# Joining the weighings of four tiles, with buffers moved between the stages, in a top-k attention and channel-mix kernel on one Trainium2 core

## The chip, the cores and the metric

The kernel runs on one core of one Trainium2 chip. A core has five engines with a queue of instructions each: TensorE (PE, matrix products and transpositions; the loading of its stationary operand is shown apart as PEld), VectorE (DVE), ScalarE (ACT), GpSimd (POOL) and SyncE (SP, which here only issues DMAs). Each engine works through its own queue in order and waits on semaphores for the others. The metric is the device time of one launch in microseconds (us); lower is better. Times are medians of several runs; the profile is of one execution.

## The reference, cut to what matters

```python
B, H, S, D = 8, 8, 576, 64          # batches, heads, positions, width of a head
scores = (q @ k.T) / sqrt(D)        # 576 x 576 for each of 64 heads
kth    = the 32nd largest of each row
scores = where(scores >= kth, scores, -1e9)
attn   = exp(scores - max);  attn = attn / (sum(attn) + 1e-9)
x      = attn @ v                   # heads side by side: 8 x 576 x 512

x_prev = x, one position later, zero first
xk = mu_k * x + (1 - mu_k) * x_prev
xr = mu_r * x + (1 - mu_r) * x_prev
h  = relu(xk @ w_k) ** 2            # 512 -> 1024
r  = 1 / (1 + exp(-(xr @ w_r)))     # 512 -> 512
out = r * (h @ w_v)                 # 1024 -> 512
```

All arrays are float32. Every matrix product of the second half is made from three products of a high and a low part (`three`, lines 703 to 705).

## The kernel before, in words

**Tiles.** Two heads are worked on together. Their 1152 rows of scores are nine tiles of 128 rows: tiles 0 to 7 hold 128 rows each of one head (even tiles the first head, odd ones the second), tile 8 the last 64 rows of both. There are 8 batches x 4 pairs of heads x 9 = 288 tiles. A batch goes over its four pairs of heads twice: first tiles 0 to 3 of each pair, then tiles 4 to 8 (`HALVES`), so there are 64 visits. The turned keys `K` of a pair are held from the first visit to the second (`HOLD`, four buffers).

**A tile's way.** PE multiplies turned queries with `K` (`score`, L990, and `sliver`, L986, which is the product with the last 64 keys; tile 8 has `score8`, L977 and L978). ACT copies the scores out of PSUM (`keep`, L995). DVE looks for the 24 largest (`cand`, `best`, `drop`: L1000, L1002, L1005) and writes two bounds into `seen` (`under`, L1012). ACT compares the scores with the bound (`count`, L1020), POOL multiplies (`below`, L1022), DVE takes the next eight (`eighth`, L1023) and from them the 32nd score (`nine`, L1025, also into `seen`). ACT makes the exponentials (L1028), and DVE masks and sums them (L1031, into `E`). PE turns `E` (`turn`, four transpositions, L1036), ACT copies the result into `et` (L1038). For every two tiles the last columns are turned together (`turnl`, L1045) and copied into `el` (L1047).

**Weighing.** `weigh` (L1066, L1067) multiplies `et` and `el` of two tiles with the values: ten products on half of the array's columns each time, for a pair of tiles. It follows every second tile, and tile 8 by itself: 160 weighings. Where `PAIR` is true, the two weighings of a group of four tiles are made as one piece of work. After a group, `place` (L1101, L1103) scales the result with the turned inverse of the sums and writes it to `xT`.

**Last keys.** The last 64 keys and, on a second visit, the last 64 queries are loaded to `tl`, turned together (L948: one transposition on a first visit, two on a second) and copied to `kd` (L950), at every visit.

**Mix.** The 4608 rows of all batches are 18 chunks of 256. For each chunk and for both mixes (k first, then r) POOL subtracts and adds (`change` L1173, `add` L1183), ACT scales (`share` L1178) and rounds to the high parts `xh` (L1185), and POOL makes the low parts `xl` (L1187, two instructions, for half of the channels each). PE then makes, in this strict order, 96 products `hidden` (256 columns, read `xl` of mix k), 24 products `gate` (512 columns, read `xl` of mix r) and 48 products `value`. POOL also squares and splits the hidden rows (L1206, L1207).

**Order.** All instructions are put in order at build time by a planner: a list of work per engine, a table of offsets by name (`OFF`, with `HEAD` and `TAIL` for the first and last tiles), costs of changing between kinds of work on PE (`SWITCH`, `LEAVE`), and the buffers of each kind (`sizes`, `MORE`). On the chip only the order and the waits are left. `seen` has two buffers, one for each of two batches; `lowest` (L1110) reads a batch's `seen` at its end.

**Weights.** In the first tiles all weights are brought in and split into high and low parts (`weight`, L1273 and on), with 80 DVE instructions in all.

## Time and profile before

| | |
|---|---|
| median of 3 runs | 1239.97 us (1239.73 to 1240.59) |
| the profiled execution, its own time | 1239.58 us |
| its span in the profile | 1238.0 us |
| busy: PE, DVE, ACT, POOL | 1185.3, 1132.4, 1107.8, 980.6 us |

The span runs from the first to the last instruction of the program; the execution's own time also holds what lies around it, 1.6 us. A busy time is the sum of what an engine works on; ends of matrix products are modelled, so that PE's busy time overlaps its own next instruction, and what PE is worth in time is read from the starts of its instructions.

### The profile page before, as it was taken

How to read it: one execution, taken by the hardware profiler on the slowest of the kernel's cores; microseconds unless marked ns; L12 is line 12 of the kernel's file. 1: busy time of each engine (PE TensorE's matmuls, PEld its weight loads, DVE VectorE, ACT ScalarE, POOL GpSimd, SP SyncE). 2: the span in 40 equal slices, each digit the busy share in tenths (PEclk: the TensorE clock that was granted, in tenths of full speed). 3: DMA queues.
4: the chain of work that ended last, by engine and by line, in shares of the span. 5: the costliest groups of instructions: out<-in, count | busy, mean ns of one | idle time of the engine just before them, and what ended most of it. 6: DMA issues, size and time to landing. Idle time of an engine off the chain costs nothing.

```text
span 1238.0 us, 29646 instructions
## 1 busy us (share of the span) xinstructions
PE 1185.3 (96%) x9069; PEld 913.8 (74%) x9069; DVE 1132.4 (91%) x6217; ACT 1107.8 (89%) x2428; POOL 980.6 (79%) x872
## 2 busy tenths in 40 slices
PE   5876999999999999999999999999999999999997
PEld 3434777878777776778787877787878787878786
DVE  5999999999999999999999999999989998999711
ACT  6897899999999999999999999999999999999752
POOL 2568995887778877888789787979697969788895
PEclk8997799999999999999999999999999999999999
DMA  7233112111221122111121112111211121101000
GB/s 189 93 95 97 35 35 66 41 36 42 57 54 31 45 50 57 36 39 45 50 56 38 35 49 58 42 43 34 59 47 45 27 59 40 50 26 32 20 27 20
DMA packets 125512, 61.80 MB, mean 50 GB/s; under 512 B 101792, under 2 KB 118176, under 8 KB 125344
## 3 DMA queue, kind: packets, MB, share of 16 engines
q1 hardware_dynamic: 124656, 59.42, 17.8%
q8 instruction: 74, 1.21, 0.4%
q14 instruction: 94, 0.77, 0.2%
q10 hardware_dynamic: 688, 0.39, 0.1%
HBM read 50.34 MB, written 9.44 MB: 48 GB/s over the span
## 4 chain that ended last, share of the span: by engine, by line
PE 79%; DVE 9%; ACT 6%; issue 1%; POOL 0%; DMA 0%; SPq 0%; DVEq 0%; ACTq 0%
PE rot L703 13%; PE rot L705 12%; PE rot L704 12%; PE ps L1066 10%; PE rot L1036 9%; PE ps L990 9%; PE ps L986 2%; PE ps L1067 2%; PE ps L977 2%; PE rot L934 2%; DVE cand L1000 2%; DVE E L1031 2%; PE rot L1088 1%; ACT sc L995 1%; PE ps L1045 1%; ACT se L1028 1%
## 5 line engine op out<-in xcount | busy, mean ns | idle before, releaser
L1022 POOL TENSOR_TENSOR sg<-sc,sg 128x576 f32<-128x576 f32 x288 | 409.2, 1423 | 165.6 <-ACT sg L1020 161.9
L1000 DVE MAX8 cand<-sc 128x8 f32<-128x82 f32 (+1 forms) x2016 | 390.5, 231 | 10.6 <-ACT sc L995 9.9
L1020 ACT ACTIVATE sg<-sc,seen 128x576 f32<-128x576 f32 x288 | 225.9, 784 | 8.6 <-DVE seen L1012 7.2
L1031 DVE SCALAR_TENSOR_TENSOR E<-sc,seen,se 128x576 f32<-128x576 f32 x288 | 231.0, 802 | 0.5 <-DVE nine L1025 0.2
L1028 ACT ACTIVATE se<-sc,seen 128x576 f32<-128x576 f32 x288 | 217.6, 756 | 8.4 <-DVE E L1031 5.8
L1023 DVE MAX8 top<-sg 128x8 f32<-128x576 f32 x288 | 215.7, 749 | 9.7 <-POOL sg L1022 9.2
L995 ACT ACTIVATE sc<-ps 128x576 f32<-128x576 f32 x288 | 185.4, 653 | 27.8 <-DVE E L1031 11.4
L1036 PE MATMUL rot<-ident,E 128*128 128x128 f32 x1152 | 180.7, 280 | 12.7 <-DVE E L1031 5.1
L1038 ACT ACTIVATE et<-rot 128x512 f32<-128x512 f32 x288 | 173.9, 604 | 9.7 <-PE rot L1036 8.6
L1002 DVE MAX8 top<-cand 128x8 f32<-128x56 f32 x864 | 179.7, 208 | 2.1
L1036 PEld LDWEIGHTS rot<-ident,E 128*128 128x128 f32 x1152 | 133.4, 143 | 62.6 <-DVE E L1031 7.1
L703 PE MATMUL rot<-xh,wk 128*128 128x256 f32 x576 | 172.5, 299 | 0.4 <-ACT kd L950 0.4
L1066 PEld LDWEIGHTS ps<-et,v 128*64 128x64 f32 x2560 | 128.7, 138 | 54.5 <-ACT el L1047 17.9
L1066 PE MATMUL ps<-et,v 128*64 128x128 f32 (+1 forms) x2560 | 164.4, 271 | 3.0 <-ACT el L1047 2.7
L705 PE MATMUL rot<-xh,wk 128*128 128x256 f32 x576 | 162.4, 282 | 0.0
L704 PE MATMUL rot<-xl,wk 128*128 128x256 f32 x576 | 162.1, 281 | 0.0
L990 PE MATMUL ps<-K,qs 64*128 64x512 f32 x512 | 149.7, 662 | 0.7 <-ACT sc L995 0.6
L703 PE MATMUL rot<-wv,hh 128*128 128x512 f32 x288 | 123.3, 428 | 0.0
L1005 DVE MATCH_REPLACE8 cand<-top,cand 128x56 f32<-128x56 f32 x576 | 115.9, 201 | 0.0
L705 PE MATMUL rot<-wv,hl 128*128 128x512 f32 x288 | 113.7, 395 | 0.0
L704 PE MATMUL rot<-wv,hh 128*128 128x512 f32 x288 | 113.6, 394 | 0.0
L703 PEld LDWEIGHTS rot<-xh,wk 128*128 128x128 f32 x576 | 109.7, 190 | 5.0 <-issue 2.4
(115 smaller groups left out, 2723.0 us busy)
## 6 DMA issues: line engine op xcount, KB each, us to landing
v<-in_v SPq DMA_DIRECT2D x64, 256.0 KB, 2.8
out<-eb SPq DMA_DIRECT2D x35, 256.0 KB, 2.0
kn<-in_k SPq DMA_DIRECT2D x64, 128.0 KB, 2.8
qn<-in_q SPq DMA_DIRECT2D x126, 64.0 KB, 2.1
stage<-in_moe_w_k SPq DMA_DIRECT2D x8, 512.0 KB, 6.2
xT<-in_moe_w_v SPq DMA_DIRECT2D x8, 512.0 KB, 3.6
tl<-in_k SPq DMA_DIRECT2D x128, 16.0 KB, 2.0
vr_in<-in_v SPq DMA_DIRECT2D x128, 16.0 KB, 2.5
```

The costliest lines, as they stand in the source:

```text
L703: return [nc.tensor.matmul(ps, lhsT=sh, rhs=mh, start=first, stop=False), nc.tensor.matmul(ps, lhsT=sh, rhs=ml, start=False, stop=False), ...
L704: nc.tensor.matmul(ps, lhsT=sh, rhs=ml, start=False, stop=False),
L705: nc.tensor.matmul(ps, lhsT=sl, rhs=mh, start=False, stop=last)]
L990: return [nc.tensor.matmul(ps[h].t, lhsT=qs.t[w, c * 128:(c + 1) * 128], rhs=P.K.t[w], start=True, stop=True) for h, w in enumerate(ws)]
L1000: lambda T=T, c=c: nc.vector.max(T.cand.t[:, 8 * c:8 * c + 8], T.sc.t[:, CUTS[c]:CUTS[c + 1]]), reads=[T.sc], writes=[(T.cand, c)])
L1020: lambda T=T, sn=sn: nc.scalar.activation(T.side.t, T.sc.t, AF.Sign, bias=sn(T, 1), scale=-BELOW, accum_out=T.top.t[:, TOPK:TOPK + 1]),
L1022: plan.op(POOL, "below", n, 1375, 1430, lambda T=T: nc.gpsimd.tensor_mul(T.side.t, T.sc.t, T.side.t), reads=[T.sc], writes=[T.side])
L1023: plan.op(DVE, "eighth", n, 660, 754, lambda T=T: nc.vector.max(T.top.t[:, 24:32], T.side.t), reads=[T.side], writes=[(T.top, 3)])
L1028: plan.op(ACT, "exps", n, 667, 754, lambda T=T, pe=pe, sn=sn: nc.scalar.activation(pe.t, T.sc.t, AF.Exp, bias=sn(T, 0), scale=SCALE), read ...
L1031: lambda T=T, U=U, pe=pe, sn=sn: nc.vector.scalar_tensor_tensor(T.e(), T.sc.t, sn(T, 2), pe.t, op0=OP.is_ge, op1=OP.mult, accum_out=U.rs.t ...
L1036: return [nc.tensor.transpose(pt.t[:, c * 128:(c + 1) * 128], E.t[:, o + c * 128:o + (c + 1) * 128], ident) for c in range(NKC)]
L1066: return [*[nc.tensor.matmul(pa[hs[j]], lhsT=vs[j][:, c, :], rhs=ms[c][j], start=(c == 0), stop=False) for c in range(NKC) for j in range(2)],
```

## The change

1. `PAIR` is true: both weighings of a group of four tiles are one piece of work, so 96 pieces in place of 160, of the same 1600 products.
2. `MORE`: `et` has five buffers in place of three, `el` three in place of two; `xl` one in place of two, `seen` one in place of two. 
3. The last 64 keys are turned once, on a pair's first visit, and held in 128 more columns of `K`; `kd` is one buffer for the last queries alone. A second visit turns and copies the queries only, and no keys are loaded on it.
4. The tables of the planner are other numbers throughout (`OFF`, `HEAD`, `TAIL`, `BONUS`, `NEAR` and others).
5. The branch for `n < WCL`, which is never taken as `WCL` is 0, is written in another way, and the constant `floor` for it is gone, one memory set on POOL.

```diff
-OFF = dict(kt=-21.382, kq=-14.248, rest=-18.039, v=-7.011, v8=8.546, tk=-6.103, ck=5.233, tq=-5.229, cq=-6.609, tr=-1.299, cr=-10.196, zero=24.959,
+OFF = dict(kt=-30.36, kq=-8.949, rest=-15.609, v=-10.829, v8=2.951, tk=-6.086, ck=4.079, tq=-5.255, cq=-6.6, tr=-1.056, cr=-7.948, zero=32.08,
...
-PAIR = False
+PAIR = True
...
-FULL = "sc", "K", "kd", "et", "el", "sg", "qs", "xm", "r", "eb", "lb", "ri"
-MORE = dict(xh=2, xl=2, et=3, top=3, el=2, qn=2, K=1 + HOLD)
+FULL = "sc", "kd", "et", "el", "sg", "qs", "xm", "r", "eb", "lb", "ri"
+MORE = {'xh': 2, 'xl': 1, 'et': 5, 'top': 3, 'el': 3, 'qn': 2, 'K': 4, 'seen': 1}
...
-            P.tl, P.kd, P.K = buf("tl"), buf("kd"), held.pop((b, hp), None)
+            P.K = held.pop((b, hp), None)
             fresh = P.K is None
+            lasts = [(k, 0)] * fresh + [(q, 128)] * full
+            P.tl, P.kd = buf("tl") if lasts else None, buf("kd") if full else None
...
-            pt, m = buf("rot"), 1 + full
-
-            def turn_t(P=P, pt=pt, m=m):
-                return [nc.tensor.transpose(pt.t[:, i * 128:(i + 1) * 128], P.tl.t[:, i * 128:(i + 1) * 128], ident) for i in range(m)]
...
+            for x, o in lasts:
+                pt, dst, last = buf("rot"), P.kd if o else P.K, "r" if o else "w"
...
-        sizes = dict(kn=(1, [128, NKC, 2, D]), qn=(1, [128, 2, 2, D]), tl=(1, [128, 256]), v=(1, [128, 2, NKC, D]), K=(2, [128, MAIN]), kd=(2, [128, 256]),
+        sizes = dict(kn=(1, [128, NKC, 2, D]), qn=(1, [128, 2, 2, D]), tl=(1, [128, 256]), v=(1, [128, 2, NKC, D]), K=(2, [128, MAIN + 128]), kd=(1, [128, 128]),
```

The tables move instructions on every engine; three places show how. In the changed kernel's rows the line numbers are one higher from `attend` on (L1067 and L1068 are the weighing, L1188 is `xl`, L1013 is `under`, L1024 is `eighth`).

PE, in the middle of the program, before: each weighing (eight products on two `et`, two on `el`) stands by itself between transpositions, scores and products of the mix.

```order
L1036 MATMUL rot2_155<-ident_59,E0_116 128x128 x4
L1066 MATMUL ps_151<-et1_123,v0_92 64x128
L1066 MATMUL ps_151<-et2_124,v0_92 64x128
...
L1067 MATMUL ps_151<-el1_126,vr_in_75 64x128 x2
L948 MATMUL rot1_154<-ident_59,tl0_91 128x128 x2
L703 MATMUL rot2_155<-wr0_70,xh1_133 128x512
...
L986 MATMUL ps_151<-kd0_97,qs0_99 128x2x64
L1045 MATMUL ps_151<-ident_59,E0_116 128x128
L990 MATMUL ps_151<-K0_93,qs0_99 128x512 x2
L1066 MATMUL ps_151<-et0_122,v0_92 64x128
L1066 MATMUL ps_151<-et1_123,v0_92 64x128
```

PE, the same part of the program, now:

```order
L705 MATMUL rot1_153<-wr0_70,xl0_135 128x512
L1067 MATMUL ps_150<-et2_122,v0_92 64x128
L1067 MATMUL ps_150<-et3_123,v0_92 64x128
...
L1068 MATMUL ps_150<-el0_125,vr_in_75 64x128 x2
L1067 MATMUL ps_150<-et4_124,v0_92 64x128
L1067 MATMUL ps_150<-et0_120,v0_92 64x128
...
L1068 MATMUL ps_150<-el1_126,vr_in_75 64x128 x2
L703 MATMUL rot1_153<-wr0_70,xh1_134 128x512
```

The second weighing of a group has moved up to the first one's end, and one change of work into a weighing and one out of it are gone.

POOL, in the last but one chunk, where `hidden` (96 products) and `gate` follow each other on PE with nothing between, before: `xl0` belongs to mix k, `xl1` to mix r, and `r` and `hl` are the hidden rows' squares and low parts.

```order
L1187 TENSOR_TENSOR xl0_134<-xm1_131,xh0_132 128x512
L1187 TENSOR_TENSOR xl1_135<-xm0_130,xh1_133 128x512
L1183 TENSOR_TENSOR xm1_131<-xm1_131,xT1_145 128x512
L1173 TENSOR_TENSOR xd00_128<-xT1_145 128x512
L1187 TENSOR_TENSOR xl1_135<-xm1_131,xh1_133 128x512
L1183 TENSOR_TENSOR xm0_130<-xm0_130,xT1_145 128x512
L1206 TENSOR_TENSOR r0_136<-r0_136 128x512
```

POOL, the same chunk, now:

```order
L1207 TENSOR_TENSOR r0_136<-r0_136 128x512
L1208 TENSOR_TENSOR hl_1325<-r0_136,hh_1287 128x512
L1207 TENSOR_TENSOR r1_137<-r1_137 128x512
L1188 TENSOR_TENSOR xl0_135<-xm0_131,xh1_134 128x512
L1188 TENSOR_TENSOR xl0_135<-xm1_132,xh1_134 128x512
L1208 TENSOR_TENSOR hl_1325<-r1_137,hh_1287 128x512
```

Both low parts of mix r stood ahead of the first hidden rows, and now stand behind the squares of the third of four, in the buffer that `hidden` reads to its end.

DVE, at the end of the fifth batch (`lowest` is the instruction that writes `least`), before: bounds of the next batch (into `seen1`) and its first `nine` and mask stand ahead of `lowest`.

```order
L1012 TENSOR_TENSOR seen1_115<-top1_108,se_152 128x2
L1000 MAX cand0_105<-sc2_103 128x8 x4
L1025 SCALAR_TENSOR_TENSOR nine0_112,seen1_115<-se_152,top0_107 128x9
L1002 MAX top2_109<-cand0_105 128x8
L1031 SCALAR_TENSOR_TENSOR E0_116,rs0_118<-sc0_101,seen1_115,se_152 128x576
...
L1012 TENSOR_TENSOR seen1_115<-top2_109,se_152 128x2
L1000 MAX cand1_106<-sc3_104 128x8 x4
L1110 TENSOR_REDUCE least_73<-seen0_114 128x1
L1002 MAX top0_107<-cand1_106 128x8
L1023 MAX top1_108<-sg1_111 128x8
```

DVE, the end of the fifth batch, now:

```order
L1003 MAX top2_108<-cand0_104 128x8
L1001 MAX cand1_105<-sc3_103 128x8 x2
L1111 TENSOR_REDUCE least_73<-seen0_113 128x1
L1013 TENSOR_TENSOR seen0_113<-top0_106,se_151 128x2
L1013 TENSOR_TENSOR seen0_113<-top1_107,se_151 128x2
L1013 TENSOR_TENSOR seen0_113<-top2_108,se_151 128x2
L1102 TENSOR_TENSOR xT0_144<-ps_150,ri0_128 128x256
L1024 MAX top0_106<-sg0_109 128x8
L1026 SCALAR_TENSOR_TENSOR nine0_111,seen0_113<-se_151,top0_106 128x9
```

The bounds of three tiles of the next batch have moved behind `lowest`, and the first `eighth` follows them with one `place` between.

## Rows read from the trace of the kernel before

**Rows 1.** The page of the profile: busy time of each engine (share of the span, instructions), and the span in 40 slices of 31 us, busy tenths of PE and DVE and the granted TensorE clock in tenths of full speed.

```profile
PE 1185.3 (96%) x9069; PEld 913.8 (74%) x9069; DVE 1132.4 (91%) x6217; ACT 1107.8 (89%) x2428; POOL 980.6 (79%) x872
...
PE   5876999999999999999999999999999999999997
...
DVE  5999999999999999999999999999989998999711
...
PEclk8997799999999999999999999999999999999999
```

**Rows 2.** Busy time by stretch: the first 36 tiles, then 18 tiles at a time (cut at every 18th mask on DVE). Columns: the stretch, its length, busy us (instructions) of PE, PEld, DVE, ACT and POOL, the granted clock, the DMA share and GB/s.

```profile
0.00:197.70 197.70, 157.39 (x968) 102.66 (x968) 182.64 (x888) 165.50 (x348) 134.32 (x124) 0.89 0.32 89
197.70:265.50 67.80, 66.54 (x522) 51.37 (x521) 66.32 (x375) 64.39 (x143) 54.86 (x49) 1.00 0.19 49
265.50:333.80 68.30, 67.37 (x561) 52.34 (x559) 67.73 (x395) 65.36 (x149) 55.23 (x51) 1.00 0.16 40
333.80:399.70 65.90, 65.46 (x515) 50.42 (x515) 64.81 (x372) 62.62 (x140) 53.76 (x47) 1.00 0.18 46
399.70:472.50 72.80, 72.30 (x596) 55.65 (x595) 70.82 (x401) 66.99 (x152) 58.20 (x56) 1.00 0.18 48
472.50:537.50 65.00, 63.80 (x490) 49.19 (x490) 63.65 (x367) 61.82 (x138) 52.02 (x45) 1.00 0.17 43
537.50:607.60 70.10, 69.74 (x575) 55.00 (x575) 69.39 (x401) 67.34 (x151) 57.19 (x54) 1.00 0.17 45
607.60:675.90 68.30, 68.02 (x530) 52.45 (x528) 67.15 (x379) 66.94 (x150) 59.13 (x50) 1.00 0.19 49
675.90:743.80 67.90, 67.25 (x546) 53.12 (x542) 66.16 (x379) 65.31 (x145) 56.70 (x51) 1.00 0.16 43
743.80:815.40 71.60, 71.39 (x576) 55.98 (x576) 68.94 (x381) 67.40 (x150) 58.78 (x54) 1.00 0.20 51
815.40:885.90 70.50, 70.30 (x578) 55.77 (x573) 68.31 (x392) 64.55 (x143) 53.49 (x49) 1.00 0.16 43
885.90:957.10 71.20, 71.20 (x567) 56.91 (x566) 67.80 (x378) 66.66 (x148) 60.24 (x53) 1.00 0.19 48
957.10:1027.10 70.00, 70.00 (x573) 55.90 (x571) 68.50 (x394) 66.60 (x151) 57.38 (x53) 1.00 0.16 40
1027.10:1102.10 75.00, 75.00 (x577) 59.06 (x576) 68.58 (x383) 68.85 (x151) 61.88 (x53) 1.00 0.15 41
1102.10:1166.90 64.80, 64.80 (x531) 51.90 (x531) 60.84 (x331) 59.14 (x131) 55.02 (x51) 1.00 0.09 26
```

**Rows 3.** The timeline of PE around one weighing and around transpositions, from answers of narrow windows (so that rows of the same products begin at several places): start, us until the last of them ends, the products, and how many rows. A product of two half-columns is two rows. The first row is four transpositions with others ahead of them, the next two rows are transpositions that follow each other; then comes a weighing with what stands ahead of it and behind it, and the copy on ACT that waits for its end.

```profile
601.40 0.60 PE L1036 MATMUL rot<-ident,E 128*128 128x128 f32 x4
...
608.45 0.27 PE L948 MATMUL rot<-ident,tl 128*128 128x128 f32 x1
608.56 0.38 PE L934 MATMUL rot<-ident,qn 128*128 128x128 f32 x2
...
605.20 0.27 PE L1045 MATMUL ps<-ident,E 128*128 128x128 f32 x1
605.40 1.09 PE L1066 MATMUL ps<-et,v 128*64 128x128 f32 x16
606.21 0.28 PE L1066 MATMUL ps<-et,v 128*64 128x128 f32 x2
606.43 0.28 PE L1067 MATMUL ps<-el,vr_in 128*64 128x128 f32 x2
606.64 0.65 PE L1036 MATMUL rot<-ident,E 128*128 128x128 f32 x4
606.76 0.28 ACT L1047 ACTIVATE el<-ps 128x128 f32<-128x128 f32 x1 [0.31 <-PE ps L1067]
```

**Rows 4.** Groups of instructions by line: count | busy us, mean ns of one | idle time of the engine just before them, and what ended most of it.

```profile
L948 PE MATMUL rot<-ident,tl 128*128 128x128 f32 x96 | 23.0, 294 | 0.8 <-ACT et L1038 0.6
...
L950 ACT ACTIVATE kd<-rot 128x256 f32<-128x256 f32 x32 | 12.4, 388 | 0.9 <-PE rot L948 0.6
L950 ACT ACTIVATE kd<-rot 128x128 f32<-128x128 f32 x32 | 8.9, 279 | 2.1 <-PE rot L948 1.9
...
L1066 PE MATMUL ps<-et,v 128*64 128x128 f32 (+1 forms) x2560 | 164.4, 271 | 3.0 <-ACT el L1047 2.7 <-DMA v<-in_v 0.2
L1101 DVE TENSOR_TENSOR xT<-ps,ri 128x256 f32<-128x256 f32 x64 | 26.6, 416 | 3.2 <-PE ps L1067 0.9 <-POOL xm L1183 0.8 <-PE ps L1045 0.6
L1020 ACT ACTIVATE sg<-sc,seen 128x576 f32<-128x576 f32 x288 | 225.9, 784 | 8.6 <-DVE seen L1012 7.2 <-DVE top L1023 0.7
L1022 POOL TENSOR_TENSOR sg<-sc,sg 128x576 f32<-128x576 f32 x288 | 409.2, 1423 | 165.6 <-ACT sg L1020 161.9 <-DVE rs L1078 1.2
L1187 POOL TENSOR_TENSOR xl<-xm,xh 128x512 fp32r<-128x512 f32 x72 | 92.4, 1288 | 9.2 <-ACT xh L1185 8.7
```

**Rows 5.** The timeline of PE where `hidden` ends and `gate` begins, in the last but one chunk.

```profile
1186.35 0.28 PE L705 MATMUL rot<-xh,wk 128*128 128x256 f32 x1
1186.46 0.40 PE L703 MATMUL rot<-wr,xh 128*128 128x512 f32 x1
1186.70 0.40 PE L704 MATMUL rot<-wr,xh 128*128 128x512 f32 x1
1186.93 0.40 PE L705 MATMUL rot<-wr,xl 128*128 128x512 f32 x1
```

More of the change, by code (lines that the diff above doesn't have):

```diff
@@ L46 @@
-CANDS, BESTS = 0.045, -0.62
-LAG, STEP, WAT, WSTEP, GATE, VALUE, PACE = 10.811, 15.812, 0.678, 0.755, 7.749, 14.045, -2.0
+OFF = dict(kt=-30.36, kq=-8.949, rest=-15.609, v=-10.829, v8=2.951, tk=-6.086, ck=4.079, tq=-5.255, cq=-6.6, tr=-1.056, cr=-7.948, zero=32.08,
+           score=-0.239, score8=-20.241, keep=-1.227, cand=5.068, best=-4.94, drop=-38.448, under=-2.732, nb=8.16, count=2.281, below=1.036,
+           eighth=6.204, nine=7.952, exps=2.736, mask=1.619, turn=3.274, et=4.281, turnl=3.599, el=4.345, weigh=1.315, inv=-0.179, inv2=-2.049,
+           turni=-0.717, ri=1.545, place=-0.114, lowest=16.268, ranks=15.011, mu=-9.72, nmu=11.088, changek=11.181, sharek=-4.663, addk=-17.151,
+           xhk=-0.124, xlk=-36.256, changer=-14.501, sharer=13.216, addr=3.351, xhr=6.025, xlr=-10.909, hidden=2.112, relu=-16.109, sq=3.703,
+           r2=7.857, hl=-4.972, gate=2.109, gexp=3.719, ga=14.142, ln=-0.365, inv1=3.697, newton=-7.448, value=0.016, scaled=-11.324, gated=-14.688,
+           store=6.787, w=19.186, wabs=-0.791, wclamp=0.38, wshift=-12.234, wsign=-0.223, wexp=-0.608, wfine=1.734, whi=4.534, wmul=13.044,
+           wsub=-11.3, wlo=2.053, spread=3.6, sliver=-2.225, low=1.195, lowt=-15.053, lowr=-7.264, lowc=-4.621, wcp=4.081, tw=-1.316, cw=-5.326)
@@ L78 @@
 WINDOW, PHASE, WARM, COLD = 3413.0, 2079.0, 0.87, 0.58
-NEAR = dict(PE=182, ACT=165, DVE=28, POOL=271, SP=294)
+NEAR = dict(PE=179, ACT=165, DVE=70, POOL=255, SP=502)
 LAST, JOINT, PEAT = "last", True, 112
-LWAT, LWSTEP = -2.585, 1.51
-LAG0, LAG1 = 8.92, 24.398
+LWAT, LWSTEP = -2.585, 2.032
+LAG0, LAG1 = 8.928, 21.018
 WPE = 12
-HEAD = dict(sharek=3.354, ck=-3.568, zero=6.524, lowt=3.202, score8=0.214, ga=4.843, store=3.315, el=0.191, gate=0.108, wlo=0.364, tr=-0.131,
-            turni=-1.056, sq=3.388, ln=-4.07, hl=-5.431, changer=2.017, relu=-14.934, wmul=-1.439, low=4.872, xhk=0.716, inv=2.094, v=4.81,
-            gated=-1.266, xlk=12.101, turn=0.113, r2=0.637, xlr=-10.187, inv1=4.923, addr=1.519, ri=-4.935, below=-1.831, scaled=-5.097, best=-1.072,
-            wabs=-0.847, lowr=-0.696, sliver=-1.103, tk=-0.128, nmu=-3.551, kq=3.958, changek=2.107, count=-0.05, hidden=-1.273, addk=-5.101,
-            xhr=2.146, lowc=-0.428, cq=0.701, eighth=-1.645, w=1.074, nb=-2.325, kt=-7.062, wshift=-2.765, wexp=0.003, ranks=8.978, rest=-10,
-            spread=5.051, mask=-0.34, whi=0.196, newton=-10.373, drop=-2.508, gexp=-0.274, keep=-0.268, tq=-0.017, inv2=3.214, mu=-5.036, weigh=0.017,
-            cr=-1.986, turnl=0.004, score=-0.211, under=-2.424, v8=2.951, nine=0.151, place=1.785, sharer=3.985, et=0.015, wfine=-0.129, wsign=1.009,
-            exps=-0.306, wsub=-1.021, lowest=-1.465, value=0.017, wcp=-0.278)
@@ new lines @@
+TAIL = dict(addr=0.752, cr=6.179, wshift=-8.106, wexp=-0.11, scaled=0.662, sq=1.94, lowt=6.719, sliver=0.582, nb=6.942, whi=-1.871, xlk=5.101,
+            xhk=0.502, store=-3.628, nine=0.364, best=-3.826, wclamp=0.405, ck=0.384, rest=5.134, lowr=4.324, ln=-2.134, hl=1.187, turni=-5.76,
+            xhr=-5.121, relu=-2.122, kt=1.207, v8=-1.721, drop=-11.981, gate=-0.057, score8=-0.335, eighth=1.269, under=6.494, inv2=2.597, v=-4.345,
+            w=0.776, wmul=-0.461, wfine=1.649, cq=-0.985, lowest=-6.351, gexp=-1.913, score=1.65, sharek=-3.769, wabs=5.934, exps=-1.268, nmu=0.127,
+            below=0.883, changek=3.97, tr=2.192, lowc=0.651, tq=-0.608, wsub=1.386, inv=0.341, low=-2.528, gated=2.636, turnl=1.258, place=5.888,
+            ri=-4.68, r2=5.232, weigh=0.964, spread=-4.571, kq=3.552, cand=0.342, value=0.283, hidden=-0.65, newton=6.002, changer=-0.142,
+            zero=-9.234, ranks=-5.673, mu=3.263, count=2.888, mask=5.945, tk=1.356, wsign=-0.204, xlr=2.939, wlo=-5.428, inv1=0.571, keep=-1.619,
+            addk=3.912, ga=-2.335, el=-0.372, sharer=-0.742, wcp=-4.705, turn=-0.055, tw=1.994, cw=2.428, et=-0.256)
```

64 lines of the change are left out of this document (29 added, 35 removed).

## The prediction

> **What bounds the kernel now.** I read the page first: PE 96% busy, DVE 91%, ACT 89%, POOL 79%, and in the slices PE and DVE both stand at 9 from about 155 us to 1150 us, with PE alone busy in the last two [rows 1]. Two engines that full may both be the bound, so the next view is the stretches of 18 tiles [rows 2]. In the eight from 197.7 to 743.8 us DVE is idle for 1.5, 0.6, 1.1, 2.0, 1.4, 0.7, 1.2 and 1.7 us (length less busy), 10.1 us in all, and PE for 0.3 to 1.3 us each. In the six from 743.8 to 1166.9 us DVE is idle for 2.7, 2.2, 3.4, 1.5, 6.4 and 4.0 us, 20.1 us in all, and PE for 0.2 us or nothing. So the first eight are bound by both engines with nearly nothing to spare on either, the last six by PE. The first 197.7 us, where the weights are split, are bound by DVE and the start: PE is idle there for 40 us and its clock is at 0.89 [rows 2]. Behind the last mask PE works off two chunks of the mix that wait for the last tiles.
>
> PE's busy time does not say that PE is full, since a matrix product's row overlaps the next. The starts do: transpositions that follow each other start 0.11 us apart [rows 3], and the waits charged to the weighing lines come to 3.0 us over the whole span [rows 4]. *A page speaks against this reading.* The Trainium skill (Perfetto Trace Analysis, Identifying the Most-Contended Engine) says that matmul busy time is no measure of the headroom of TensorE and that the busy share of weight loading is to be taken. By that rule PE stands at 74% [rows 1] with a quarter to spare, DVE is the bound, and what PE saves is worth nothing; that is the second rival below. By the spacing of the starts PE has nothing to spare after 744 us, and I go by that.
>
> **The change part by part.**
>
> *Joined weighings.* What a weighing costs beside its ten products can be read off [rows 3]. Inside, product follows product every 0.11 us (606.21 and 606.43 are the starts of the last but two and of the last). The last one holds PE until 606.64, 0.21 us, so leaving costs 0.10. From 605.40 to 606.21 lie seven starts: 0.81 - 7 x 0.109 = 0.05 more for the first. Into it, the transposition at 605.20 is followed after 0.20 in place of 0.11: 0.09. Behind it, four transpositions take 0.65 in place of 0.60 (606.64 against 601.40): 0.05. The order of the change has 96 weighings in place of 160, so 64 x (0.10 + 0.05) = 9.6 us go. The changes into a weighing or a score from other work fall from 203 to 188 in the two orders (a joined weighing's neighbours now often meet at a score instead), 15 x 0.09 = 1.4. First pieces of other work behind either fall by 15 as well, at 0.05: 0.8. Together 11.8 us of PE.
>
> *Last keys kept turned.* 32 transpositions (L948, 96 to 64) at 0.11 us [rows 3, 4] are 3.5 us of PE. On ACT 32 copies of 256 columns become 32 of 128: 32 x (0.388 - 0.279) = 3.5 us [rows 4], beside other work, as ACT is not the bound in any stretch [rows 2]: nothing. 64 small loads leave SP's queue, which no row of the argument waits for: nothing. PE's sum is 11.8 + 3.5 = 15.3 us over 16 stretches of 18 tiles, 0.96 us each.
>
> *What of that reaches the end.* In the first 36 tiles nothing: DVE has the same instructions to do there. Later a stretch can shrink by 0.96 us only as far as DVE's idle time lets it. I take the smallest idle time that any stretch shows, 0.6 us, as what DVE cannot shed. The eight early ones then give 0.9, 0, 0.5, 0.96, 0.8, 0.1, 0.6, 0.96 = 4.8 us, the six late ones 5 x 0.96 + 0.9 = 5.7 us: 10.5 us together. The bounds are nothing, if DVE's idle time is all made of its own pipeline's waits, and 15.3 us.
>
> *Five `et`, three `el`.* They let the copies of a group stand until the joined weighing. All that PE waited at the weighing is 3.0 us [rows 4]; the first half of a joined one reads copies that are long made. Inside the 0.6 us floor above: no term of its own, between 0 and 3 us of gain.
>
> *One `xl`.* Mix r's low parts can now be written only when the last `hidden` product has read mix k's. In chunks 17 and 18 `gate` follows `hidden` at once. Before, the last `hidden` product starts at 1186.35 and the first reader of mix r's `xl` at 1186.93 [rows 5]. Now the reader comes after the product's end (1186.35 + 0.28), POOL's 1.29 us [rows 4] and two hand-overs between engines; one that can be read is 0.05 us, from the weighing's end at 606.71 to ACT's copy at 606.76 [rows 3]. That is 1188.02, 1.1 us later. Two chunks: 2.2 us, nothing to hide it. It is at least 2 x (1.29 - 0.58) = 1.4 us, if POOL needs not wait for the product's modelled end, and 5.0 us if a `below` or its like (1.42 us) is under way on POOL each time. In the other 16 chunks the order has at least 1.7 us of attention work on PE between the two (a score, a sliver, four transpositions), which with 0.5 us to the first reader covers 1.9 us, if POOL is free at that moment. POOL then has both `xl` (2.6 us) ahead of the next tiles' `below`, and a `below` that is under way holds them for up to 1.42 us [rows 4]. I take 1.0 us for all 16, nearest to a cover that mostly holds; the bounds are 0 and 16 x 1.42 = 22.7 us, with no gain, since a buffer less moves nothing forward.
>
> *One `seen`.* The next batch's bounds wait for `lowest`. From a bound to its `eighth` lie `count` 0.78 and `below` 1.42 [rows 4], 2.2 us, and a little over with `under` itself. At the first four ends of a batch the new order has 3.3 to 6.4 us of DVE work between the two (my count of its instructions by their durations), so nothing is exposed. At the fifth to the seventh only one or two bounds and a `place` (0.42 us [rows 4]) stand there: DVE waits about 1.9, 1.9 and 1.5 us. Those fall into the stretches from 743.8, 885.9 and 1027.1 us, where DVE has 2.7, 3.4 and 6.4 us idle as it is [rows 2]. Taking 0.6 + 1.9 as the floor, only the first two lose some of their gain: 0.8 us. The bounds are 0 and 5.3 us.
>
> *Rest.* Writing the untaken branch otherwise and one memory set less change nothing. The weights' splitting on DVE ends nine tiles later in the new order, 80 instructions as before; the first product of the mix stands one tile earlier, and by the 36th tile as many products are done (168 against 156 in the two orders). I take 0, with 2 us to either side for the start.
>
> *Sum*, against the execution's own time: 1239.6 - 10.5 + 2.2 + 1.0 + 0.8 = 1233.1 us. Its own time stands 0.4 us under the median of the runs, so a median would be 1233.1 to 1233.5; I say 1233.3.
>
> **The rivals.**
>
> *All of PE's saving arrives.* DVE's floor is not 0.6 us, as the longer buffers also take away its waits. 1239.6 - 15.3 + 1.4 to 2.2 = 1225.7 to 1226.5. For it: the smallest idle times stand where PE was late least. Against: the first 36 tiles cannot give any.
>
> *DVE binds, and PE waits for what it saved.* PE's 0.96 us a stretch turns into idle time of PE, since DVE's own chain (score, count, `below`, `eighth`) sets the pace of a tile; only the two exposed `xl` remain: 1239.6 + 2.2 = 1241.8 us, and 1240 if some of the late stretches give. For it: DVE idles 1 us in 67 early on. Against: the six late stretches, in which PE has no idle time and DVE has 20.1 us [rows 2].
>
> *POOL holds up DVE (slower).* In the 16 chunks in mid-program the two `xl` wait at the head of POOL's queue for the last `hidden`, and then hold the next `below` for 2.6 us; `eighth`, `nine` and the mask wait behind it, the turning of that tile behind the mask. It decides from 0.65 us a chunk: without the 1.0 us taken above the sum is 1232.1, and 16 x 0.65 = 10.4 us take it to 1242.5. At half of a `below`, 0.7 us, the time is 1232.1 + 11.2 = 1243.3 us; at a whole one 1254.8. For it: POOL works in order, is 85% busy in a stretch [rows 2], and today waits for ACT alone at `xl`. Against: DVE has up to four tiles' scores to go on with, and POOL's idle time at `below`, 166 us [rows 4], is mostly room.
>
> That the weighings are not joined at all is excluded by the order.
>
> **How the numbers follow.** The forecast, part of PE's saving (1228 to 1238): 0.50. All of it (1225 to 1228): 0.12. DVE binds (1238 to 1242.5): 0.20. POOL holds up DVE (over 1242.5): 0.18. Faster or slower by over 0.2% is under 1237.5 or over 1242.4 us, about what a measurement of this kernel can tell from no change. Faster takes the first two, 0.62; the same the third, 0.20; slower the last, 0.18. The range from 1226 to 1244 leaves out the lowest end of the second and more than half of the last.
>
> **What would show it.** Right: a weighing's line with 0.10 us of leaving in 96 places; DVE's idle time in the late stretches cut by 5 us or so, and the last mask at about 1157 us in place of 1167; PE idle for 1.3 us ahead of the third `gate` product in each of the last two chunks, and nowhere else. Wrong: the late stretches as long as before with PE idle in them (DVE bound), idle time of DVE at `eighth` released by POOL wherever two `xl` stand together in mid-program (POOL), or a first 36 tiles that are more than 2 us off.

## The result, and the profile after

The changed kernel takes 1248.24 us (median of 4 runs, 1247.43 to 1248.35), the kernel before 1239.85 us on the same chip (4 runs, 1239.25 to 1240.59). The ratio is 1.0064, 95% interval 1.0050 to 1.0078: 8.4 us slower. The forecast was 1233.3 us in a range from 1226 to 1244, so the time lies 4.2 us above the range and on the other side of no change. The profiled execution shown here takes 1248.29 us, 1246.5 us of it span.

The page of the changed kernel: busy time of each engine, and the chain of work that ended last, by engine.

```profile
PE 1183.5 (95%) x9037; PEld 911.0 (73%) x9037; DVE 1136.9 (91%) x6217; ACT 1108.3 (89%) x2428; POOL 980.5 (79%) x871
...
PE 61%; DVE 21%; ACT 13%; POOL 2%; issue 2%; SPq 1%; DMA 1%; ACTq 0%; DVEq 0%; POOLq 0%
```

The second of these lines on the page of before, which the prediction did not read:

```profile
PE 79%; DVE 9%; ACT 6%; issue 1%; POOL 0%; DMA 0%; SPq 0%; DVEq 0%; ACTq 0%
```

Before, four fifths of the chain are PE's own work, and DVE and ACT have 15%; now they have a third (21% and 13%). Busy time hardly shows this: PE's 1183.5 us stand against 1185.3 [rows 1], only 1.8 us less where 15.3 were forecast. Its ends are modelled, so it does not tell what PE saved.

Busy time by stretch after, cut at the same masks as [rows 2], with stretches put together (length; PE, PEld, DVE, ACT, POOL busy and instructions; clock; DMA share; GB/s).

```profile
0.00:204.80 204.80, 161.69 (x1005) 106.00 (x1007) 187.57 (x902) 168.91 (x354) 134.46 (x124) 0.90 0.32 89
204.80:680.10 475.30, 466.36 (x3720) 361.61 (x3717) 468.42 (x2657) 451.93 (x1008) 388.70 (x346) 0.99 0.17 44
680.10:754.40 74.30, 72.33 (x579) 55.62 (x578) 70.19 (x405) 68.03 (x152) 57.90 (x51) 1.00 0.16 39
754.40:1175.40 421.00, 418.40 (x3353) 332.34 (x3354) 401.63 (x2239) 390.50 (x864) 347.27 (x311) 1.00 0.15 41
1175.40:1246.50 71.10, 64.75 (x397) 55.44 (x391) 9.10 (x20) 28.88 (x53) 52.18 (x43) 0.99 0.06 21
```

Against [rows 2]: the first 36 tiles take 204.8 us in place of 197.7 (+7.1); the next seven stretches 475.3 in place of 478.2 (-2.9); the stretch with the end of the fifth batch 74.3 in place of 67.9 (+6.4); the last six 421.0 in place of 423.1 (-2.1); what lies behind the last mask 71.1 both times. That is +8.5 us, all of it ahead of the last mask. Work has moved between the stretches as well, so a stretch's own difference is not a loss: in the one with the end of the fifth batch DVE is busy for 4.0 us more than before (70.2 against 66.2, with 405 instructions against 379) and idle for 2.4 us more (4.1 against 1.7).

The second row hides one place. Right behind the first 36 tiles PE waits 1.99 us for a mask, and by 208 us the granted clock is at 0.50, which is the 1.2 GHz level, up to about 214 us. The timeline of PE there:

```profile
205.68 0.66 PE L1037 MATMUL rot<-ident,E 128*128 128x128 f32 x4 [0.38 <-DVE E L1032]
...
208.73 1.11 PE L1037 MATMUL rot<-ident,E 128*128 128x128 f32 x4 [1.99 <-DVE E L1032]
```

The same place in stretches, then the 18 tiles that begin with it and 18 tiles further on (columns as above; the clock is the third number from the end):

```profile
208.00:210.00 2.00, 1.27 (x6) 1.23 (x7) 2.00 (x9) 2.00 (x6) 1.03 (x1) 0.50 0.15 33
210.00:214.00 4.00, 4.00 (x14) 1.95 (x12) 4.00 (x25) 3.95 (x10) 2.57 (x3) 0.50 0.00 0
...
204.80:269.70 64.90, 60.48 (x473) 45.99 (x470) 63.66 (x369) 62.05 (x137) 53.77 (x46) 0.95 0.12 31
...
340.70:405.60 64.90, 64.08 (x508) 49.65 (x508) 64.15 (x369) 62.98 (x143) 53.91 (x47) 1.00 0.17 44
```

Four transpositions take 1.11 us at this clock and 0.66 us just before. In the same 64.9 us PE has 35 rows fewer than in the later stretch at full clock; at 64.9 / 508 us a row this is an estimate of 4.5 us of work put off by the waits and the clock together, though the rows of the two are not all alike. The kernel before has clock 1.00 in every stretch behind its start [rows 2]. How much of the 4.5 us reaches the end no run shows.

What was sized well is the joined weighing itself. The timeline of PE around one, after (start, length, products, rows; the first row has only the beginning of the first weighing's products):

```profile
707.57 0.66 PE L1067 MATMUL ps<-et,v 128*64 128x128 f32 x8
...
709.58 0.39 PE L1068 MATMUL ps<-el,vr_in 128*64 128x128 f32 x4
709.90 0.66 PE L1037 MATMUL rot<-ident,E 128*128 128x128 f32 x4
```

From 707.57 to the next work at 709.90 are 2.33 us for twenty products; a single one took 606.64 - 605.40 = 1.24 us [rows 3]. So 2 x 1.24 - 2.33 = 0.15 us are saved here, as the prediction had it; the joined weighing at 750.20 us takes 2.34 us.

At the ends of the late batches DVE waits, as the prediction expected of one `seen`. The timeline of DVE at the end of the fifth batch, after, and in the last row the `below` that the first `eighth` (L1024) reads; in brackets the idle time ahead of an instruction and what ended it:

```profile
750.02 0.21 DVE L1111 TENSOR_REDUCE least<-seen 128x1 f32<-128x72 f32 x1
750.27 0.29 DVE L1013 TENSOR_TENSOR seen<-top,se 128x2 f32<-128x2 f32 x3
752.90 0.42 DVE L1102 TENSOR_TENSOR xT<-ps,ri 128x256 f32<-128x256 f32 x1 [2.35 <-PE ps L1046]
753.25 0.75 DVE L1024 MAX8 top<-sg 128x8 f32<-128x576 f32 x1
...
751.40 1.42 POOL L1023 TENSOR_TENSOR sg<-sc,sg 128x576 f32<-128x576 f32 x1
```

Three bounds of the next batch stood back until `lowest` had read the old ones, and their `count` and `below` (to 752.82) have to come before the first `eighth`. DVE idles 2.35 us; 1.9 were expected. The wait is charged to the `place`, whose joined weighing holds PE from 750.20 to 752.54, but without the `place` the `eighth` could begin only at 752.82 in place of 753.25, 0.4 us sooner. At the end of the sixth batch DVE idles 1.15 and 0.72 us; 1.9 were expected there too. ACT waits more for DVE in the whole program (groups by line after; the waits ended by the bounds, L1013, and by `eighth`, L1024, were 7.2 and 0.7 us [rows 4]):

```profile
L1021 ACT ACTIVATE sg<-sc,seen 128x576 f32<-128x576 f32 x288 | 225.1, 782 | 16.1 <-DVE seen L1013 11.9 <-DVE top L1024 3.3
```

### The profile page after: what moved, and what is told of

It is laid out like the page before. It is cut to its first block, busy times and chain, and to the rows that moved or that the text cites. A ratio compares the mean times of both kernels' runs of the same rounds, so it can differ in the third digit from the quotient of the medians.

```text
span 1246.5 us, 29496 instructions
## 1 busy us (share of the span) xinstructions
PE 1183.5 (95%) x9037; PEld 911.0 (73%) x9037; DVE 1136.9 (91%) x6217; ACT 1108.3 (89%) x2428; POOL 980.5 (79%) x871
## 4 chain that ended last, share of the span: by engine, by line
PE 61%; DVE 21%; ACT 13%; POOL 2%; issue 2%; SPq 1%; DMA 1%; ACTq 0%; DVEq 0%; POOLq 0%
PE rot L703 11%; PE rot L705 10%; PE rot L704 10%; PE ps L1067 7%; PE rot L1037 7%; PE ps L991 6%; DVE cand L1001 5%; DVE E L1032 4%; DVE top L1024 3%; ACT sc L996 2%; ACT sg L1021 2%; DVE top L1003 2%; PE ps L987 2%; ACT se L1029 2%; DVE cand L1006 2%
## 5 line engine op out<-in xcount | busy, mean ns | idle before, releaser
L1024 DVE MAX8 top<-sg 128x8 f32<-128x576 f32 x288 | 215.6, 749 | 7.0 <-POOL sg L1023 6.4
L704 PE MATMUL rot<-xl,wk 128*128 128x256 f32 x576 | 162.5, 282 | 0.0
L705 PE MATMUL rot<-xh,wk 128*128 128x256 f32 x576 | 162.2, 282 | 0.0
L1067 PE MATMUL ps<-et,v 128*64 128x128 f32 (+1 forms) x2560 | 158.7, 266 | 1.1 <-ACT el L1048 0.9
L1067 PEld LDWEIGHTS ps<-et,v 128*64 128x64 f32 x2560 | 130.2, 137 | 29.0 <-issue 9.3
L705 PE MATMUL rot<-wv,hl 128*128 128x512 f32 x288 | 113.8, 395 | 0.0
L704 PE MATMUL rot<-wv,hh 128*128 128x512 f32 x288 | 113.6, 394 | 0.0
```

What stands on the lines that cost most here:

```text
L704: nc.tensor.matmul(ps, lhsT=sh, rhs=ml, start=False, stop=False),
L705: nc.tensor.matmul(ps, lhsT=sl, rhs=mh, start=False, stop=last)]
L1024: plan.op(DVE, "eighth", n, 660, 754, lambda T=T: nc.vector.max(T.top.t[:, 24:32], T.side.t), reads=[T.side], writes=[(T.top, 3)])
L1067: return [*[nc.tensor.matmul(pa[hs[j]], lhsT=vs[j][:, c, :], rhs=ms[c][j], start=(c == 0), stop=False) for c in range(NKC) for j in range(2)],
```

## The experiments

The times of before vary between 1239.2 and 1240.1 us over the calls; each ratio is against the runs of before in its own call.

### Which engine bounds: work cut out in the kernels' own order

In the weighing (b_pe of before, a_pe of the changed kernel; the output lacks a fourth of the main columns):

```diff
-                        return [*[nc.tensor.matmul(pa[hs[j]], lhsT=vs[j][:, c, :], rhs=ms[c][j], start=(c == 0), stop=False) for c in range(NKC) for j in range(2)],
+                        return [*[nc.tensor.matmul(pa[hs[j]], lhsT=vs[j][:, c, :], rhs=ms[c][j], start=(c == 0), stop=False) for c in range(NKC - 1) for j in range(2)],
```

In the mask (b_dve, a_dve; the last 96 columns are not made):

```diff
-                        lambda T=T, U=U, pe=pe, sn=sn: nc.vector.scalar_tensor_tensor(T.e(), T.sc.t, sn(T, 2), pe.t, op0=OP.is_ge, op1=OP.mult, accum_out=U.rs.t[:, T.i - U.i:T.i - U.i + 1]),
+                        lambda T=T, U=U, pe=pe, sn=sn: nc.vector.scalar_tensor_tensor(T.e()[:, :480], T.sc.t[:, :480], sn(T, 2), pe.t[:, :480], op0=OP.is_ge, op1=OP.mult, accum_out=U.rs.t[:, T.i - U.i:T.i - U.i + 1]),
```

b_pe: 

> The kernel before, in its own order, with two of the eight wide products of every weighing left out (the fourth part of the main columns is not added), so the output lacks that part. PE loses 128 x 2 x 0.109 + 32 x 2 x 0.06 = 32 us of products, 0.11 us a tile, and no other engine loses anything. If PE bounds the last six stretches, as the prediction had it, these 108 tiles give 11 us or so, and the whole 12 to 20 us. If DVE bounds the kernel all through, the time falls by less than 4 us and PE waits for the rest.

b_dve: 

> The kernel before, in its own order, with the mask made over 480 of its 576 columns (the last 96 columns of the turned exponentials are left as they were, two buffers being set to zero at the start). DVE loses 288 x 0.1 = 29 us, 0.10 us a tile, and no other engine loses anything. If DVE bounds the kernel all through, 20 to 29 us go. If PE bounds the last six stretches, only the first ten can give, under 18 us, and those from 744 us on stay as long as they are.

a_pe: 

> The changed kernel, in its own order, with the same two products of every weighing left out: 32 us less on PE. The changed kernel already has 46 us of PE waiting between 130 and 1150 us. If DVE bounds it, the time falls by less than 3 us. If its waits on PE are what lengthens it (a place that waits for a joined weighing at the end of a batch), the shorter weighing gives 2 x 0.22 us at each of the seven ends and some of it elsewhere, 4 to 8 us.

a_dve: 

> The changed kernel, in its own order, with the mask made over 480 of its 576 columns, as in the other kernel: 29 us less on DVE. If DVE bounds it, 20 to 29 us go, at least as much as in the kernel before, since its PE has more to spare. If waits between engines bound it, under 15 us.

Measured: b_pe 1224.79 us (ratio 0.9889, 0.9873 to 0.9906), b_dve 1238.34 (0.9991, 0.9981 to 1.0001), a_pe 1238.66 (0.9993, 0.9983 to 1.0002), a_dve 1244.52 (1.0042, 1.0027 to 1.0056). Of 32 us cut from PE, 14.6 arrive before and 9.6 after the change; of 29 us cut from DVE, 1.1 before (its interval reaches no change) and 3.7 after. DVE does not bind the kernel before, although it is 91% busy: the 0.10 us a tile that it is given come back as idle time. PE does, but no cut of it arrives whole. What keeps the other half was not tried; no cut was made on ACT (89% busy) or POOL (79%). By stretch in b_pe:

```profile
197.20:735.30 538.10, 528.74 (x3997) 403.47 (x3995) 532.44 (x3057) 518.72 (x1158) 446.64 (x397) 1.00 0.18 46
735.30:1152.20 416.90, 415.26 (x3153) 323.52 (x3153) 400.27 (x2254) 391.06 (x869) 346.65 (x311) 1.00 0.16 42
```

The early eight stretches give 8.0 us (546.1 to 538.1), the late six 6.2 (423.1 to 416.9), out of 2.0 us cut in each stretch. Half is the yield early and late; "both engines early, PE late" was the wrong picture, and the 11 us or so expected of the late six did not come, though the whole lies in the expected 12 to 20. a_pe gave more than the 4 to 8 us expected. Here the measurement also decides on the page that the prediction set against itself. The Trainium skill (Perfetto Trace Analysis, Identifying the Most-Contended Engine) judges the headroom of TensorE by its share of the peak rate and by the busy share of weight loading, the latter 74% here, by which DVE at 91% is the most contended engine. The runs do not agree: a cut on DVE is worth about a twelfth of one on PE in the kernel before.

### Parts undone, the tables left as they were

In the changed kernel, pairoff has

```diff
-PAIR = True
+PAIR = False
```

oldtab has the tables of before (`OFF`, `HEAD`, `TAIL` and the numbers beside them), newtab is the kernel before with the changed tables, and wtab takes eleven offsets of the weights' splitting and its due times from before (and, by 0.05 at most, the offsets `GATE` and `VALUE`); the planner makes an order for each.

pairoff: 

> The changed kernel with the two weighings of a group apart again; tables, buffers and turned last keys stay as changed, and the order is worked out anew. If the joined weighing is what makes PE wait (it holds PE for 2.3 us, and the batch's last place waits for all of it), the late batch ends lose their 3 to 5 us of waiting each and the time falls by 5 us or more, although PE gets 64 boundaries back. If the joining saves PE time and the loss comes from elsewhere (the start, the tables), the time rises by 3 to 10 us.

oldtab: 

> The changed kernel with the tables of numbers of the kernel before (the two new offsets take the values that the joint one had): joined weighings, five et, three el, one xl, one seen, last keys kept turned. If the tables cost the time (the order of the start above all), it comes to 1238 to 1243 us and the 36th mask is back at 198 us. If the structure costs it, it stays at 1246 us or above, with a start as before and late stretches as long as in the changed kernel.

newtab: 

> The kernel before with the tables of numbers of the changed one: weighings apart, three et, two xl, two seen. If the tables cost the time, the 36th mask is at 203 us or later, and the time is 1245 us or more. If the structure costs it, the time is within 4 us of 1239.5.

wtab: 

> The changed kernel with the eleven offsets of the weights' splitting and their due times taken from the kernel before, nothing else. The splitting then ends on DVE behind mask 19 in place of 29. If the 7 us that the first 36 tiles are longer are lost to the end, the 36th mask comes at 198 us and the time at 1241 to 1243 us. If they are given back later (the changed kernel has 12 rows more of the mix done by then, and PE is the bound behind it), the 36th mask comes earlier and the time stays at 1246 to 1250 us.

Measured: 1270.87 us (1.0246), 1280.30 (1.0326), 1268.49 (1.0233) and 1274.26 (1.0277), each interval within 0.0021 to either side. pairoff and wtab miss both of their expectations; oldtab and newtab lie on the side that one theory gave them, but so far beyond it (1246 and 1245 us or more) that they don't bear it out. All four stand 20 to 41 us above both kernels, though each undoes or takes over only a part of the change. They say nothing of the parts. What they show is what an order costs that is made with tables not fitted to its structure: against the same structure with fitted tables pairoff is 16.9 us longer (t_pairoff, below), wtab 26.0, newtab 28.4 and oldtab 32.1, more than any part turns out to be worth. A part can only be judged with tables fitted to it.

### Parts alone, each with its tables searched again

For the next kernels the tables were searched for half an hour to forty minutes each: numbers in `OFF`, `HEAD`, `TAIL` and `BONUS` were moved at random, and what made the planner's order shorter by its own costs was kept. t_before is before searched in that way, t_after the changed kernel. Against t_before, b_x1 and b_s1 differ in one buffer each, x1s1 in both:

```diff
-MORE = dict(xh=2, xl=2, et=3, top=3, el=2, qn=2, K=1 + HOLD)
+MORE = dict(xh=2, xl=1, et=3, top=3, el=2, qn=2, K=1 + HOLD, seen=1)
```

(b_x1 leaves out `seen=1`, b_s1 keeps `xl=2`.)

t_before: 

> The kernel before with nothing changed but the tables that set its order: a search moved their numbers for 40 minutes and kept what made the order shorter by the planner's own costs. It is the measure for the next three, whose tables were searched in the same way for the same time. If the tables of before were already as good as such a search makes them, 1236 to 1241 us; if there was more to find, 1230 to 1236 us.

b_x1: 

> The kernel before with one buffer for the mix's low parts in place of two and nothing else of the change, the order searched anew as for t_before. If one buffer costs what the prediction put on it (1.0 us in mid-program and 2.2 us at the tail), 2 to 4 us over t_before. If it is what eats the joined weighings' gain, because the gate's products can no longer be fed while the hidden products run and the order of the whole has to give way, 8 to 14 us over t_before. If it costs nothing, within 1 us.

b_s1: 

> The kernel before with one buffer for the bounds seen in place of two and nothing else of the change, the order searched anew as for t_before. If it costs what the prediction put on it (0.8 us, covered by DVE's idle time), within 2 us of t_before. If the end of every batch holds up the next one's bounds, and with them the scores on all engines, 4 to 8 us over t_before.

t_after: 

> The changed kernel with nothing changed but the tables that set its order, searched for 40 minutes as for t_before, from its own. If its loss is a poor order (the start above all), the search mends it and the time falls to t_before or below. If the buffers of the change bound it, the search finds nothing and the time stays within 3 us of 1248, 8 us or more over t_before.

x1s1: 

> The kernel before with one buffer for the low parts and one for the bounds seen, nothing else of the change, the order searched as for t_before. If the two costs add (12.6 and 9.4 us over t_before), about 1262 us; the joined weighings, kept keys and longer chain of turned tiles of the changed kernel would then be worth 14 us, which is the saving on PE that was forecast. If they overlap, 1250 to 1256 us, and the rest of the change is worth little.

Measured: t_before 1240.24 us (1.0006, 0.9996 to 1.0015), b_x1 1252.87 (1.0111, 1.0094 to 1.0128), b_s1 1249.68 (1.0081, 1.0064 to 1.0097), t_after 1248.91 (1.0075, 1.0059 to 1.0092), x1s1 1254.47 (1.0123, 1.0106 to 1.0140). A new search moves neither kernel by more than 0.8 us; as far as such a search can tell, the loss is not a poor order. One buffer for the low parts costs 12.6 us, one for the bounds 9.4 (more than the 4 to 8 expected), both 14.2: they overlap. These three began from tables that were fitted to two buffers, so a poorer fit may have a part in their price; that it is a large one is unlikely, as t_pairoff (below) was searched from the changed kernel's tables and comes to the same time as x1s1, 1254.0 and 1254.5 us, though its kept keys and further `et` and `el` differ too. In x1s1 the loss is time that PE loses between the end of the first 36 tiles and the last mask. The windows of t_before and then of x1s1 for that stretch:

```profile
199.60:1163.20 963.60, 959.60 (x7690) 752.56 (x7685) 938.51 (x5315) 908.46 (x2023) 791.08 (x704) 1.00 0.17 44
```

```profile
201.60:1179.60 978.00, 965.56 (x7701) 754.73 (x7700) 942.49 (x5297) 914.44 (x2025) 794.18 (x706) 1.00 0.17 43
```

PE stands idle for 4.0 us in the first and 12.4 in the second, and its rows lie further apart (6.0 us more busy for 11 rows more). For `xl` little of it is a wait for the buffer itself. The writes of the low parts on POOL in b_x1, and on the last line in the changed kernel, wait 2.3 and 1.3 us for PE in the whole program:

```profile
L1187 POOL TENSOR_TENSOR xl<-xm,xh 128x512 fp32r<-128x512 f32 x72 | 91.5, 1284 | 4.6 <-PE rot L704 2.3 <-ACT xh L1185 1.7
```

```profile
L1188 POOL TENSOR_TENSOR xl<-xm,xh 128x512 fp32r<-128x512 f32 x72 | 91.6, 1288 | 3.1 <-ACT xh L1186 1.5 <-PE rot L704 1.3
```

So the price of one `xl` is in the order. How it arises is read from the order and was not tried by itself: with one buffer the gate's low parts cannot be made ahead of the last hidden product, and attention work has to be kept back to stand between the two, in every chunk.

For `seen` it is otherwise: the wait itself can be seen. The 8 us behind each of the first seven `lowest`, seven windows put together, in t_before and then in b_s1:

```profile
sum 56.00, PE 55.54 PEld 42.92 DVE 52.52 ACT 52.88 POOL 44.48; mean PE 7.93 PEld 6.13 DVE 7.50 ACT 7.55 POOL 6.35
```

```profile
sum 56.00, PE 54.71 PEld 41.48 DVE 45.06 ACT 50.63 POOL 41.44; mean PE 7.82 PEld 5.93 DVE 6.44 ACT 7.23 POOL 5.92
```

DVE is idle for 10.9 us there in place of 3.5, while PE goes on (1.3 us idle in place of 0.5). DVE's 7.4 us more are of the size of the 9.4 us that b_s1 is longer. Whether the price comes by way of this wait or of the order around it is not shown.

### The rest of the change alone

kept holds the last keys turned, with one `kd` in place of two as in the change, and alters no other buffer; t_pairoff is the changed kernel with `PAIR = False` and its tables searched; c5a joins the weighings with both pairs of buffers kept and four `et`, c8 with five, c8k with the kept keys besides:

```diff
-PAIR = False
+PAIR = True
...
-MORE = dict(xh=2, xl=2, et=3, top=3, el=2, qn=2, K=1 + HOLD)
+MORE = dict(xh=2, xl=2, et=5, top=3, el=3, qn=2, K=1 + HOLD, lb=2, eb=2)
```

(that is c8; c5a has `et=4` and leaves `eb` at three, c8k has `el=2`.)

kept: 

> The kernel before with the last keys kept turned and nothing else of the change, the order searched as for t_before. The forecast put 3.5 us of PE on it, about half of which can arrive by what a cut on PE brought: 1237 to 1240 us. If the split into two transpositions and copies costs as much as it saves, 1240 to 1243 us.

t_pairoff: 

> The changed kernel with the two weighings of a group apart again (buffers and kept keys as changed), the order searched as for t_after. If the joining brings what it saves on PE (11.8 us), some 5 to 12 us over t_after's 1248.9. If joined weighings themselves hold things up, at or below t_after.

c5a: 

> The kernel before with joined weighings and four places for turned exponentials, three for their last parts, both buffers for the low parts and both for the bounds as before; the room comes from two in place of three buffers for the gate's logarithm, which moved nothing in the order of before. The order is searched as for t_before. If the joining is worth its saving on PE once no buffer is taken away, 1228 to 1237 us. If it is not, or if four places are too few, 1240 to 1246 us.

c8: 

> The kernel before with joined weighings and five places for turned exponentials, three for their last parts, both buffers for the low parts and both for the bounds; the room comes from the gate's buffers, two each in place of three for its exponentials and its logarithms. The order is searched as for t_before. If joining is worth its saving on PE once no buffer that attention or the hidden products wait for is taken away, 1230 to 1237 us. If joining is worth nothing by itself, 1238 to 1245 us.

c8k: 

> As c8, and the last keys kept turned, with two places for the last parts: the whole change, its room taken from the gate's buffers. If the kept keys bring part of their 3.5 us, 1 to 3 us under c8. If they cost what they did alone (4.1 us over t_before), 2 to 5 us over c8.

Measured: kept 1244.32 us (1.0037, 1.0023 to 1.0052), t_pairoff 1253.99 (1.0128, 1.0111 to 1.0146), c5a 1239.17 (0.9999, 0.9989 to 1.0008), c8 1241.33 (1.0015, 1.0006 to 1.0024), c8k 1249.52 (1.0084, 1.0072 to 1.0096). At the changed buffers joining gives 5.1 us (t_after under t_pairoff). Where its room comes from the gate's buffers it comes to 1.1 us under t_before in c5a and 1.1 over it in c8; the intervals of each overlap with t_before's, so neither difference is clear of the noise. kept, c5a and c8k lie outside all that was expected of them. In c8 PE is idle for 10.9 us between the end of the first 36 tiles and the last mask, 6.9 more than in t_before:

```profile
200.90:1168.90 968.00, 957.14 (x7705) 756.16 (x7703) 940.36 (x5314) 910.13 (x2026) 794.71 (x707) 1.00 0.17 44
```

So PE's busy time is 2.5 us less, for 15 rows more, and its idle time takes that back and more. The lower clock of the changed kernel has a part in these comparisons that no run sets apart: t_after, c5a and c8 have a place at clock 0.50 between 207 and 218 us, of 3 to 7 us, while t_before, x1s1, kept, t_pairoff and c8k stand at 1.00 from 190 to 1160 us. The kept keys did not gain in either pair (4.1 us over t_before, 8.2 over c8, which also has an `el` more); how much of that is their own, how much the second `kd` that they give up, and how much an order that the search left poor is open. No version beats the kernel before.

## Why the prediction was wrong, step by step

The ledger, from the searched kernels: one `xl` and one `seen` +14.2 us (x1s1 against t_before), five `et`, three `el` and kept keys -0.5 (t_pairoff against x1s1), joining -5.1 (t_after against t_pairoff). By construction they add up to t_after's 8.7 over t_before; the changed kernel is 8.4 over before. The middle step is within the spread of the runs (t_pairoff's lie between 1253.4 and 1257.9 us), and there the search also began from other tables, so what five `et`, three `el` and the kept keys are worth one by one is open. The ledger is also taken from one side only. c8k has the joined weighings and the kept keys with both pairs of buffers back (and two `el`, fewer buffers for the gate): it takes 1249.5 us, no less than t_after's 1248.9. So the runs show that the kernel before loses 14.2 us without the two buffers; that the changed kernel would win its 8.4 us back with them they do not show.

- **"One `xl`" and "One `seen`" are the steps that failed** as far as the runs show: 1.0 + 2.2 + 0.8 = 4.0 us in the sum, 14.2 us measured in the kernel before. They were priced as waits at the buffer, and the waits came about as expected; the step from the wait to the time failed. At the tail the third gate product starts 0.86 us behind the second in place of 0.23, 0.63 us late in each of two chunks (the lower bound was 0.7 each, the value taken 1.1), as the timeline of PE shows:

```profile
1194.51 0.39 PE L703 MATMUL rot<-wr,xh 128*128 128x512 f32 x1
1194.74 0.40 PE L704 MATMUL rot<-wr,xh 128*128 128x512 f32 x1
1195.60 0.50 PE L705 MATMUL rot<-wr,xl 128*128 128x512 f32 x1 [0.46 <-POOL xl L1188]
```

  It is a little under the bound because the last product of `hidden` reads `xh` (L705); `xl` is free one product earlier, at L704, and POOL begins to write it at 1194.27 us, ahead of that last product (1194.40), which the prediction overlooked. The stretch behind the last mask is no longer for it, 71.1 us both times. In the whole program POOL waits 1.3 us for PE at `xl`. What the prediction missed is that the order is made anew around the missing buffer, and that PE loses time all over (12.4 us idle in x1s1 against 4.0); that the order is bent to avoid the waits is how I read it, not shown. For one `xl` the bounds (up to 22.7 and 5.0 us) held and the value taken stood at their lower end. For one `seen` the waits of the fifth and sixth batch came as forecast (2.4 and 1.9 us), but the prediction let DVE's idle time swallow all but 0.8 us; 9.4 us alone is beyond even the bound of 5.3.
- **"What of that reaches the end"** was too much: 10.5 of 15.3 us. A cut of PE in the order of before arrives to 14.6 / 32 = 46%, which would make 7.0; joining, 11.8 us of it, gave 5.1 us at the changed buffers, and nothing that stands clear of the noise where its room came from the gate's. The floor of DVE's idle time, by which the stretches were sorted, sorts them wrongly: by it the 2.0 us a stretch of b_pe would give 5.4 us in the early eight and 10.5 in the late six (the idle times of [rows 2] less 0.6 us, at most 2.0 each); they gave 8.0 and 6.2.
- **"Rest", 0 within 2 us**, was off: the first 36 tiles take 7.1 us more. PE does 4.3 us more work in them (161.7 against 157.4 busy), so some 3 are lost. Right behind them PE runs at half its clock for some 6 us, an estimate of 4.5 us of work put off, for which the prediction had no term. The mask behind the 36 tiles begins at 206.1 us in t_after and t_pairoff as well, but at 201.7, 200.9, 201.6, 203.3 and 200.6 in c5a, c8, x1s1, kept and c8k. Each part of the change stands in one of these five, so none of them brings the longer start by itself; newtab, which has the changed tables and none of the parts, begins it at 210.9. That points to the tables; it was not tried with fitted ones.
- **Joined weighings** and the **tail**: 0.15 us a boundary was right; the tail was 1.3 us in place of 2.2.
- **The rivals.** "DVE binds" is wrong as a bound (b_dve, a_dve), though its consequence, PE waiting for what it saved, is what c8 shows. "POOL holds up DVE" gave a time on the right side, 1243.3 to 1254.8 us, but the changed kernel does not show its mechanism: DVE's waits for POOL at `eighth` fell from 9.2 to 6.4 us, and POOL waits 1.3 us for PE at `xl`. Among the searched kernels these waits of DVE rise, from 3.7 us in t_before to 6.6 in b_x1 and 8.4 in x1s1, so up to 4.7 of the 14.2 us may come that way; in t_after they are 4.1. The price at which it decided, 0.65 us a chunk, was near (12.6 / 18 = 0.7), which is luck as far as the mechanism goes.

## What to carry to other kernels

Where engines follow an order that is fixed beforehand, a buffer's price can be many times the wait that is seen at it (2.3 us of waiting and 12.6 us of time for one `xl`), because the order has to change around it. Price it by making the order again without the buffer, and with the tables fitted anew, since tables made for another structure cost 17 to 32 us here. Before giving an engine's saving to the end, read the shares of the chain that ended last, and cut the same amount from that engine in the old order: 46% of a cut arrived from an engine that is 96% busy, and 4% from one that is 91% busy. Read the granted clock in short stretches too: a mean of 0.99 hid 6 us at half the clock.
